# The attention products of a fused kernel: two segments a quad over two PSUM banks instead of three pairs of passes

## The chip, the cores and the metric

The kernel runs on one core of a Trainium2 chip. The metric is the device time of one execution in microseconds; lower is better.

## The reference

Attention over 8 batches, 8 heads, 576 queries and 16 + 576 keys (16 "beacon" keys in front, always visible; the rest causal), then a feed-forward network (FFN) whose hidden layer is the maximum of three products:

```python
k_all = concatenate([beacon_k, k], axis=2); v_all = concatenate([beacon_v, v], axis=2)
scores = q @ k_all.T / sqrt(64)                 # B=8, H=8, S=576, D=64
a = softmax(where(causal, -1e9, scores))        # key n of k is seen by queries >= n
attn_out = a @ v_all
x = attn_out.transpose(0, 2, 1, 3).reshape(4608, 512)
h = maximum(maximum(x @ w1, x @ w2), x @ w3)    # 512 -> 768
return h @ w_out                                # 768 -> 512, float32
```

## The kernel before, in words

**Quads.** Four heads of one batch are a quad; there are 16 quads (`Q`), two a batch. Scores are computed transposed, keys on the partitions: five key tiles `t` of 128, 128, 128, 128 and 80 keys, of which tile `t` is seen by the queries from `q_min[t]` = 0, 112, 240, 368, 496 up to 576. One quad has 1664 visible columns a head (576 + 464 + 336 + 208 + 80).

**Steps.** The visible columns are packed into bursts of at most 512 columns. The main loop in `emit_all` has one step a burst, 55 in all, numbered `k`. Quads 0 to 3 have four bursts each, packed one by one. From quad 4 on (`N_APART`) bursts run on across quads; quad 4 begins at step 16 (`late`). A step issues, in this order:

- a part of the products of an earlier quad (`emit_pv`), if one is due;
- the score products of its burst (`emit_scores`, L272; four heads side by side on four row strips of TensorE, two halves of the head dimension), into two PSUM tiles `sc` of two banks, one for two heads;
- on ScalarE the exponential of the first two heads (`emit_exp(0)`, L287), one FFN unit, the exponential of the other two, and the causal masks on GpSimd (L303);
- the planned work of that step: transposes of later q and k on VectorE (`turn`, L199), loads, casts of v on GpSimd (L225), each followed by an FFN unit if one is allowed; then the remaining allowed FFN units.

**FFN units.** `mm1_unit` multiplies a block of 512 tokens by 128 columns of one of the three weights: four products of 512 columns (eight of 256 for block 4) into an `ffn_psum` tile. Weight 0 is copied into `hT` by ScalarE (L382, a "copy" unit), weights 1 and 2 are folded in by VectorE (L387, a "maximum" unit). `mm2_unit` is an "output" unit: six products (L394) and a copy `y` on VectorE (L402). `ffn_psum` has two buffers, so the third unit of a run waits until the first is emptied. How many units a step gets follows from rates in `emit_all` (2.6 units a step at first, 3.4 later) and from `ready`, the last batch whose attention is complete.

**Attention products (PV).** A pass (`pv_pass`) covers one half of the queries (288) and one part: part 0 multiplies by ones and gives the softmax's denominators, parts 1 and 2 multiply by the even and odd columns of v. Four heads go side by side on four column strips of TensorE (L333), summed over key tiles into a PSUM tile `pv` of one bank; the pool has two. After part 0, ScalarE makes the reciprocal as the exponential of minus the logarithm (L343, L345). After parts 1 and 2, VectorE multiplies the tile by the reciprocal into `xT` (L349), the FFN's input. The passes of a quad go in three pairs, one pair a step:

```python
            [(Q, 0, 0), (Q, 1, 0)],
            [(Q, 0, 1), (Q, 0, 2)],
            [(Q, 1, 1), (Q, 1, 2)],
```

So the first pair (32 products) is followed by two logarithms and two reciprocals; the second (24) and third (40) by two multiplies each, with reciprocals that are one or two steps old. On TensorE such a step reads: PV run, score run, FFN run.

**Queues.** Every engine works its queue in the order of issue. TensorE's first score product of a step waits for the exponentials of the step before, which empty `sc`. When the loop ends, the tail issues the pairs that are left (quad 14's third and quad 15's three, each with an FFN unit before and behind) and then all units that are left, over `ffn_psum` and `sc_psum` in turn.

Of the kernel before, what the change touches and what calls it, by code (L numbers as in the profile page):

```python
# [7 lines left out]
FP32 = mybir.dt.float32  # L8
BF16 = mybir.dt.bfloat16
U32 = mybir.dt.uint32  # L10
AF = mybir.ActivationFunctionType
ALU = mybir.AluOpType
PSUM = bass.MemoryType.PSUM
# [3 lines left out]
def kernel(  # L17
# [13 lines left out]
    nc = tc.nc  # L31

    B, H, S, D = q.shape
    Nb = beacon_k.shape[2]
    NK = S + Nb
    scale = 1.0 / float(D) ** 0.5
# [8 lines left out]
    HG = 4  # L45
    n_quad = H // HG
# [5 lines left out]
    HALF = S // 2  # L52

    n_kt = (NK + 127) // 128
    k_rows = [min(128, NK - 128 * t) for t in range(n_kt)]
    q_min = [max(0, 128 * t - Nb) for t in range(n_kt)]
# [5 lines left out]
    BANK = 512  # L62
    N_APART = 2 * n_quad
    by_burst = [
        [[(0, 0, HALF), (3, q_min[3], S)], [(1, q_min[1], S)], [(2, q_min[2], S)]]
        + [[(0, HALF, S), (4, q_min[4], S)]],
        [[(0, 0, HALF), (1, q_min[1], S), (2, q_min[2], S), (0, HALF, S)]]
        + [[(3, q_min[3], S), (4, q_min[4], S)]],
    ]
    bursts = []  # L70
    at_piece = {}
    for Q in range(NQ):
# [4 lines left out]
        for group in by_burst[0 if apart else 1]:  # L77
            if apart:
                room = 0
            for t, q0, q1 in group:  # L80
                at_piece.setdefault((Q, t), []).append((q0, q1, pos))
                while q0 < q1:
# [3 lines left out]
                    w = min(room, q1 - q0)  # L86
                    bursts[-1].append((Q, t, q0, q0 + w, pos))
                    pos, q0, room = pos + w, q0 + w, room - w
# [5 lines left out]
    RING = 4  # L94
# [6 lines left out]
    xT = xt_pool.tile([128, n_ct, RING * S], BF16)  # L101
# [6 lines left out]
    nrm_pool = ctx.enter_context(tc.tile_pool(name="nrm", bufs=2))  # L108
    ffn_h = ctx.enter_context(tc.tile_pool(name="ffn_h", bufs=2))
    ffn_y = ctx.enter_context(tc.tile_pool(name="ffn_y", bufs=3))  # L110
    sc_psum = ctx.enter_context(tc.tile_pool(name="sc_psum", bufs=2, space=PSUM))
    pv_psum = ctx.enter_context(tc.tile_pool(name="pv_psum", bufs=2, space=PSUM))
    ffn_psum = ctx.enter_context(tc.tile_pool(name="ffn_psum", bufs=2, space=PSUM))

    ones = const.tile([128, 32], BF16, name="ones")
    nc.vector.memset(ones, 1.0)
# [89 lines left out]
    v_tiles = {}  # L206
# [48 lines left out]
    at = {}  # L255
# [41 lines left out]
    def emit_masks(k):  # L297
        for Q, t, q0, q1, a in bursts[k]:
            edge = min(q1, 128 * t - Nb + k_rows[t])
            if edge > q0:  # L300
                n = k_rows[t]
                view = at[Q][0:n, :, a : a + edge - q0]
                nc.gpsimd.affine_select(  # L303
                    out=view,
                    in_=view,
                    compare_op=ALU.is_ge,
                    fill=0.0,
                    base=q0 - (128 * t - Nb),
                    pattern=[[0, HG], [1, edge - q0]],
                    channel_multiplier=-1,  # L310
                )
# [3 lines left out]
    def pv_pass(Q, hf, part):  # L315
        b, g = divmod(Q, n_quad)
        at_sb, v_sb = at[Q], v_tiles[b]
        h0, h1 = hf * HALF, (hf + 1) * HALF
        runs = []
        for t in range(n_kt):  # L320
            for q0, q1, a in at_piece[Q, t]:
                lo, hi = max(q0, h0), min(q1, h1)
                if lo < hi:
                    runs.append((t, lo, hi, a + lo - q0))
        ps = pv_psum.tile([128, HALF], FP32, name="pv")
        for i, (t, lo, hi, a) in enumerate(runs):
            n = k_rows[t]
            for j in range(HG):
                if part == 0:
                    lhsT = ones[0:n, :]  # L330
                else:
                    lhsT = v_sb[0:n, t, HG * g + j, part - 1 : D : 2]
                nc.tensor.matmul(  # L333
                    ps[32 * j : 32 * j + 32, lo - h0 : hi - h0],
                    lhsT,
                    at_sb[0:n, j, a : a + hi - lo],
                    start=(i == 0),
                    stop=(i == len(runs) - 1),
                    tile_position=(0, 32 * j),
                )  # L340
        if part == 0:
            lnd = nrm_pool.tile([128, HALF], FP32, name="lnd")
            nc.scalar.activation(out=lnd, in_=ps, func=AF.Ln)  # L343
            recip = nrm_pool.tile([128, HALF], FP32, name="recip")
            nc.scalar.activation(out=recip, in_=lnd, func=AF.Exp, scale=-1.0)  # L345
            recips[Q, hf] = recip
        else:
            c0 = b % RING * S + h0
            nc.vector.tensor_mul(xT[:, 2 * g + part - 1, c0 : c0 + HALF], ps, recips[Q, hf])  # L349


    def pv_pairs(Q):
        return [
            [(Q, 0, 0), (Q, 1, 0)],
            [(Q, 0, 1), (Q, 0, 2)],
            [(Q, 1, 1), (Q, 1, 2)],
        ]

    def emit_pv(passes):
        for one in passes:  # L360
            pv_pass(*one)

# [75 lines left out]
    def emit_ffn(limit, ready, pool=None, name="fps"):  # L438
        if done[0] + 1 <= limit and done[0] < len(units) and units[done[0]][0] <= ready:
            _, fn, args = units[done[0]]  # L440
            fn(*args, pool or ffn_psum, name)
            done[0] += 1
            return True
        return False
# [15 lines left out]
    def begin():  # L460
        load_first_beacon_k(0, nc.scalar)
        load_qk(0, 1, (0, SH, QS))
        load_qk(0, 0, (0, SH, QS))
        load_qk(1, 1, (0, QS))
        load_qk(1, 0, (0, QS))
        load_first_beacon_k(1, nc.sync)
        load_v(0)
        load_beacon_k(1, 2, nc.sync)
        for which, s0, s1 in ((1, 0, SH), (1, SH, QS), (0, 0, SH), (0, SH, QS)):
            cast_qk(0, which, by_act, s0, s1)  # L470
            if (which, s0) == (0, SH):
                turn_first_beacon_k(0)
            turn(0, which, s0, s1)
        cast_qk(1, 1, by_dve)
        turn(1, 1, 0, SH)
        turn(1, 1, SH, QS)
        turn_first_beacon_k(1)
        cast_qk(1, 0, by_pool)
# [16 lines left out]
    for Q in range(2, NQ):  # L495
        b, g = divmod(Q, n_quad)
# [16 lines left out]
    def emit_all():  # L513
        begin()
        ready = -1
        allowed = 0.0


        late = first_step[2 * n_quad]
        early_rate = 2  # L520
        first_rate, rate = 2.6, 3.4
        pairs = []
        for k in range(N_STEP):
            Q = bursts[k][0][0]
            if k == late:

                while pairs:
                    emit_pv(pairs.pop(0))
                    emit_ffn(n_ft * 3, ready)
                ready = 1  # L530
                allowed += 2
            pair = ()
            if k == n_quad * 4:
                pair = pairs.pop(0)
            elif pairs and k < late and k % 4 > 0:
                pair = pairs.pop(0)
            elif pairs and k > max(late, last_step[pairs[0][0][0]] + 1):

                pair = pairs.pop(0)

            if Q >= n_quad:
                emit_pv(pair)
            emit_exp = emit_scores(k)
            if k > late and pair and pair[-1][0] % n_quad == n_quad - 1 and pair[-1][1:] == (1, 2):
                ready = pair[-1][0] // n_quad
            if k >= late:
                allowed += rate if ready > 1 else first_rate
            elif k >= n_quad * 4:
                allowed += early_rate

            emit_exp(0)
            emit_ffn(allowed, ready)
            emit_exp(1)
            emit_masks(k)
            if Q < n_quad:
                emit_pv(pair)
            if k == n_quad * 4:
                while pairs:
                    emit_pv(pairs.pop(0))
                ready = 0  # L560
            for fn in plan.pop(k, ()):
                fn()
                emit_ffn(allowed, ready)
            while emit_ffn(allowed, ready):
                pass
            if k == last_step[Q]:
                pairs += pv_pairs(Q)
        assert not plan, list(plan)
        for pair in pairs:
            emit_ffn(len(units), B - 2)  # L570
            emit_pv(pair)
            emit_ffn(len(units), B - 2)
        i = 0
        tail = [(ffn_psum, "fps"), (sc_psum, "sc")]
        while emit_ffn(len(units) - 1, B - 1, *tail[i % 2]):
            i += 1
        last_unit(*units[-1][2], (tail[i % 2], tail[(i + 1) % 2]))

    with tc.manual_schedule():
        emit_all()  # L580
# [30 lines left out]
```

## Time and profile before

| | us |
|---|---|
| median of 3 runs | 294.62 |
| lowest and highest | 294.28, 294.78 |
| profiled execution, whole | 294.3 |
| its span in the profile | 292.6 |

Of the span TensorE is busy 94%, VectorE 58%, ScalarE 54%, GpSimd 30%, at full granted clock. In the profile PE is TensorE, DVE VectorE, ACT ScalarE and POOL GpSimd. A row of a timeline has the start in the span, the length, the engine, the line of the kernel, the operation, output and input, the count, and in brackets the idle time before it and what ended that. A row of a group has busy time and mean length in ns after the first bar. A row of the waits has, after who waited for whom, the total, the number of times and the longest. A row of a window table has, for each engine, busy time and number of instructions, then the granted clock.

### The profile page before, as it was taken

How to read it: one execution, taken by the hardware profiler on the slowest of the kernel's cores; microseconds unless marked ns; L12 is line 12 of the kernel's file. 1: busy time of each engine (PE TensorE's matmuls, PEld its weight loads, DVE VectorE, ACT ScalarE, POOL GpSimd, SP SyncE). 2: the span in 40 equal slices, each digit the busy share in tenths (PEclk: the TensorE clock that was granted, in tenths of full speed). 3: DMA queues.
4: the chain of work that ended last, by engine and by line, in shares of the span. 5: the costliest groups of instructions: out<-in, count | busy, mean ns of one | idle time of the engine just before them, and what ended most of it. 6: DMA issues, size and time to landing. Idle time of an engine off the chain costs nothing.

```text
span 292.6 us, 8225 instructions
## 1 busy us (share of the span) xinstructions
PE 275.1 (94%) x3534; PEld 141.6 (48%) x3534; DVE 169.8 (58%) x297; ACT 157.2 (54%) x246; POOL 88.5 (30%) x165
## 2 busy tenths in 40 slices
PE   0697999999999999999999999999999999999995
PEld 0245445544455454545546777445454554444442
DVE  2717769756656565756646566657552545555553
ACT  5698575467872848368563756384828430220210
POOL 0474862235624423153323441332132200000000
PEclk9999999999999999999999999999999999999999
DMA  7899999589935944259057905390031002103003
GB/s 246 223 176 208 131 182 199 90 181 228 210 59 157 211 76 81 75 142 182 2 83 216 176 3 83 121 193 4 0 110 38 2 0 107 39 0 138 7 1 143
DMA packets 51924, 33.08 MB, mean 113 GB/s; under 512 B 41264, under 2 KB 42288, under 8 KB 51888
## 3 DMA queue, kind: packets, MB, share of 16 engines
q1 hardware_dynamic: 41152, 20.40, 26.5%
q0 software_dynamic: 10464, 12.01, 25.8%
q8 instruction: 27, 0.44, 0.6%
q10 hardware_dynamic: 272, 0.15, 0.2%
q14 instruction: 9, 0.07, 0.1%
HBM read 35.13 MB, written 9.44 MB: 152 GB/s over the span
## 4 chain that ended last, share of the span: by engine, by line
PE 84%; ACT 10%; DVE 2%; DMA 2%; issue 1%; SPq 0%; DVEq 0%
PE fps L374 40%; PE fps L394 14%; PE pv L333 12%; PE sc L272 10%; PE sc L374 5%; ACT at_sb L287 5%; PE sc L394 2%; ACT lnd L343 2%; DMA st<-in_q_dram 2%; ACT recip L345 1%; ACT hT L382 1%; DVE qT L199 1%; DVE hT L387 0%; DVE xT L349 0%; SPq L182 0%
## 5 line engine op out<-in xcount | busy, mean ns | idle before, releaser
L374 PE MATMUL fps<-xT,w_sb 128*128 128x512 bf16 (+1 forms) x648 | 138.6, 356 | 1.5 <-ACT hT L382 1.3
L287 ACT ACTIVATE at_sb<-sc 128x1024 bf16<-128x1024 f32 (+7 forms) x128 | 104.3, 863 | 60.6 <-PE sc L272 60.4
L387 DVE TENSOR_TENSOR hT<-hT,fps 128x512 bf16<-128x512 bf16 x96 | 65.8, 686 | 70.5 <-PE fps L374 50.4
L374 PEld LDWEIGHTS <-w_sb 128*128 128x128 bf16 x720 | 66.5, 98 | 71.1 <-issue 10.5
L303 POOL TENSOR_SCALAR_AFFINE_SELECT at_sb<-at_sb 128x512 bf16<-128x512 bf16 (+5 forms) x89 | 47.6, 551 | 132.8 <-ACT at_sb L287 124.4
L272 PE MATMUL sc<-qT,kT 32*128 32x288 bf16 (+16 forms) x1056 | 41.6, 260 | 11.7 <-DVE qT L199 9.3
L382 ACT CAST hT<-fps 128x512 bf16<-128x512 f32 x42 | 24.7, 587 | 41.8 <-PE fps L374 41.8
L394 PE MATMUL fps<-w_out_sb,hT 128*128 128x512 bf16 x180 | 41.8, 379 | 0.0
L272 PEld LDWEIGHTS <-kT 32*128 32x128 bf16 x1056 | 21.7, 94 | 28.6 <-issue 13.3
L402 DVE COPY y<-fps 128x512 f32<-128x512 f32 x30 | 20.8, 692 | 19.9 <-PE fps L394 19.8
L349 DVE TENSOR_TENSOR xT<-pv,recip 128x288 bf16<-128x288 f32 x64 | 27.0, 450 | 9.1 <-PE pv L333 8.8
L394 PEld LDWEIGHTS <-hT 128*128 128x128 bf16 x210 | 19.9, 98 | 24.4 <-DVE hT L387 1.6
L333 PE MATMUL pv<-at_sb,v_sb 128*32 128x288 bf16 (+4 forms) x1024 | 29.3, 256 | 0.4 <-DVE xT L349 0.4
L333 PEld LDWEIGHTS <-v_sb 128*32 128x32 bf16 (+1 forms) x1024 | 21.6, 97 | 14.3 <-issue 11.1
L199 DVE STREAM_TRANSPOSE kT<-c 128x256 uint32<-128x256 uint32 (+1 forms) x32 | 22.0, 706 | 3.5 <-ACT c L192 3.4
L199 DVE STREAM_TRANSPOSE qT<-c 128x256 uint32<-128x256 uint32 (+1 forms) x32 | 21.8, 706 | 0.8 <-ACT c L192 0.8
L374 PE MATMUL sc<-xT,w_sb 128*128 128x512 bf16 x72 | 18.5, 379 | 0.0
L343 ACT ACTIVATE lnd<-pv 128x288 f32<-128x288 f32 x32 | 12.9, 403 | 7.1 <-PE pv L333 7.1
L333 PE MATMUL pv<-at_sb,ones 128*32 128x288 bf16 (+4 forms) x512 | 15.2, 261 | 0.6 <-DVE xT L349 0.6
L225 POOL CAST v_sb<-vst 128x1024 bf16<-128x1024 f32 (+1 forms) x18 | 15.7, 894 | 0.1
L345 ACT ACTIVATE recip<-lnd 128x288 f32<-128x288 f32 x32 | 14.2, 444 | 1.0
L333 PEld LDWEIGHTS <-ones 128*32 128x32 bf16 (+1 forms) x512 | 10.6, 98 | 8.5 <-issue 5.2
(35 smaller groups left out, 67.9 us busy)
## 6 DMA issues: line engine op xcount, KB each, us to landing
out_dram<-y SPq DMA_DIRECT2D x35, 256.0 KB, 2.0
vst<-in_v_dram SPq DMA_DIRECT2D x21, 256.0 KB, 4.9
c<-in_k_dram POOLq DMA_DIRECT2D x14, 288.0 KB, 5.3
c<-in_q_dram POOLq DMA_DIRECT2D x14, 288.0 KB, 6.2
w_sb<-in_moe_w_dram POOLq DMA_DIRECT2D x3, 768.0 KB, 9.0
vst<-in_v_dram SPq DMA_DIRECT2D x7, 224.0 KB, 3.7
vst<-in_v_dram SPq DMA_DIRECT2D x7, 160.0 KB, 5.9
w_out_sb<-in_moe_w_out_dram POOLq DMA_DIRECT2D x1, 768.0 KB, 10.8
```

The source lines that it names most:

```text
L199: nc.vector.transpose(dst.rearrange("p (t s) -> p s t", s=RUN)[:, s0:s1], src.rearrange("p (s d) -> p s d", d=DP),)
L272: nc.tensor.matmul(sc[h // 2][:, h % 2, off : off + w], kT[hs, 128 * t : 128 * (t + 1), j], qT[hs, q0:q1, j], start=(j == 0), stop=(j == 1 ...
L287: nc.scalar.activation(out=at[Q][:, 2 * i : 2 * i + 2, a0 : a0 + w], in_=sc[i][:, :, off : off + w], func=AF.Exp, scale=scale,)
L303: nc.gpsimd.affine_select(out=view, in_=view, compare_op=ALU.is_ge, fill=0.0, base=q0 - (128 * t - Nb), pattern=[[0, HG], [1, edge - q0]], ...
L333: nc.tensor.matmul(ps[32 * j : 32 * j + 32, lo - h0 : hi - h0], lhsT, at_sb[0:n, j, a : a + hi - lo], start=(i == 0), stop=(i == len(runs) ...
L343: nc.scalar.activation(out=lnd, in_=ps, func=AF.Ln)
L349: nc.vector.tensor_mul(xT[:, 2 * g + part - 1, c0 : c0 + HALF], ps, recips[Q, hf])
L374: nc.tensor.matmul(ps[:, o0 : o0 + n], w_in[i][:, ct, 128 * ft : 128 * (ft + 1)], xT[:, ct, x0 : x0 + n], start=(ct == 0), stop=(ct == n_c ...
L382: nc.scalar.copy(hT[:, ft, :], ps)
L387: nc.vector.tensor_max(hT[:, ft, :], hT[:, ft, :], ps)
L394: nc.tensor.matmul(ps, hT[:, ft, 128 * tt : 128 * (tt + 1)], w_out_sb[:, ft, :], start=(ft == 0), stop=(ft == n_ft - 1),)
L402: nc.vector.tensor_copy(y, ps)
```

## The change

For quads 4 to 15 the three pairs become two segments, one a step: queries 0 to 240 and queries 240 to 576 (`SPLIT = q_min[2]`). A segment holds all three parts, side by side in one PSUM tile of two banks (`pv2`, one buffer in place of the two of `pv`, whose pool is closed ahead of it). In segment 0 part 0 lies at columns 0 to 240, part 1 at 240 to 480 and part 2 in the second bank; in segment 1 they lie at 0, 336 and 672, and part 1 is cut where it crosses into the second bank. Segment 0 has 24 products (key tiles 0 and 1), segment 1 has 76. TensorE posts one semaphore a segment, at its last product; the logarithm waits for that. The two multiplies (`finish`) are issued after the step's first exponential, and `ready` rises after them. The scores of these quads are packed tile by tile, so that key tile 0 is one piece and not two halves; there are 960 score products instead of 1056. Quads 0 to 3 keep their passes. The steps keep their FFN units; the steps that held a third pair have no PV run now. On TensorE's queue there are 135 unbroken runs of one kind (PV, scores, FFN), against 149.

```diff
-        [[(0, 0, HALF), (1, q_min[1], S), (2, q_min[2], S), (0, HALF, S)]]
-        + [[(3, q_min[3], S), (4, q_min[4], S)]],
+        [[(t, q_min[t], S) for t in range(n_kt)]],
...
+    def pv_segment(Q, seg):
+        b, g = divmod(Q, n_quad)
+        at_sb, v_sb = at[Q], v_tiles[b]
+        h0, h1 = ((0, SPLIT), (SPLIT, S))[seg]
+        n = h1 - h0
+        offs = (0, n, BANK) if seg == 0 else (0, n, 2 * n)
+        if len(pv_pool) == 1:
+            pv_stack.close()
+            pv_pool.append(ctx.enter_context(tc.tile_pool(name="pv2_psum", bufs=1, space=PSUM)))
+        pv_banks = pv_pool[1].tile([128, 2 * BANK], FP32, name="pv2")
+        for part in range(3):
+            runs = []
+            for t in range(n_kt):
+                ((q0, q1, a),) = at_piece[Q, t]
+                lo = max(q0, h0)
+                c = offs[part] + lo - h0
+                c1 = offs[part] + n
+                while lo < h1 and c < c1:
+                    w = min(c1, (c // BANK + 1) * BANK) - c
+                    runs.append((t, c, w, a + lo - q0))
+                    lo, c = lo + w, c + w
+            for i, (t, c, w, a) in enumerate(runs):
+                r = k_rows[t]
+                for j in range(HG):
...
+                    nc.tensor.matmul(
+                        pv_banks[32 * j : 32 * j + 32, c : c + w],
+                        lhsT,
+                        at_sb[0:r, j, a : a + w],
+                        start=(t == 0),
+                        stop=all(x[1] // BANK != c // BANK for x in runs[i + 1 :]),
+                        tile_position=(0, 32 * j),
+                    )
+        lnd = nrm_pool.tile([128, S - SPLIT], FP32, name="lnd")[:, 0:n]
+        nc.scalar.activation(out=lnd, in_=pv_banks[:, 0:n], func=AF.Ln)
+        recip = nrm_pool.tile([128, S - SPLIT], FP32, name="recip")[:, 0:n]
+        nc.scalar.activation(out=recip, in_=lnd, func=AF.Exp, scale=-1.0)
+        c0 = b % RING * S + h0
+
+        def finish():
+            for part in (1, 2):
+                nc.vector.tensor_mul(
+                    xT[:, 2 * g + part - 1, c0 : c0 + n],
+                    pv_banks[:, offs[part] : offs[part] + n],
+                    recip,
+                )
+
+        return finish
...
     def pv_pairs(Q):
+        if Q >= N_APART:
+            return [[(Q, 0)], [(Q, 1)]]
...
+            finish = None
             if Q >= n_quad:
-                emit_pv(pair)
+                finish = emit_pv(pair)
             emit_exp = emit_scores(k)
-            if k > late and pair and pair[-1][0] % n_quad == n_quad - 1 and pair[-1][1:] == (1, 2):
-                ready = pair[-1][0] // n_quad
...
             emit_exp(0)
+            if finish:
+                finish()
+                if pair[-1][0] % n_quad == n_quad - 1 and pair[-1][1] == 1:
+                    ready = pair[-1][0] // n_quad
             emit_ffn(allowed, ready)
             emit_exp(1)
...
         for pair in pairs:
             emit_ffn(len(units), B - 2)
-            emit_pv(pair)
+            emit_pv(pair)()
             emit_ffn(len(units), B - 2)
```

More of the change, by code (lines that the diff above doesn't have):

```diff
@@ L111 @@
     sc_psum = ctx.enter_context(tc.tile_pool(name="sc_psum", bufs=2, space=PSUM))
-    pv_psum = ctx.enter_context(tc.tile_pool(name="pv_psum", bufs=2, space=PSUM))
     ffn_psum = ctx.enter_context(tc.tile_pool(name="ffn_psum", bufs=2, space=PSUM))
+    pv_stack = ExitStack()
+    pv_pool = [pv_stack.enter_context(tc.tile_pool(name="pv_psum", bufs=2, space=PSUM))]
     ones = const.tile([128, 32], BF16, name="ones")
@@ L324, in pv_pass @@
                     runs.append((t, lo, hi, a + lo - q0))
-        ps = pv_psum.tile([128, HALF], FP32, name="pv")
+        ps = pv_pool[0].tile([128, HALF], FP32, name="pv")
         for i, (t, lo, hi, a) in enumerate(runs):
@@ L341, in pv_pass @@
         if part == 0:
-            lnd = nrm_pool.tile([128, HALF], FP32, name="lnd")
+            lnd = nrm_pool.tile([128, S - SPLIT], FP32, name="lnd")[:, 0:HALF]
             nc.scalar.activation(out=lnd, in_=ps, func=AF.Ln)
-            recip = nrm_pool.tile([128, HALF], FP32, name="recip")
+            recip = nrm_pool.tile([128, S - SPLIT], FP32, name="recip")[:, 0:HALF]
             nc.scalar.activation(out=recip, in_=lnd, func=AF.Exp, scale=-1.0)
@@ L349, in pv_pass @@
             nc.vector.tensor_mul(xT[:, 2 * g + part - 1, c0 : c0 + HALF], ps, recips[Q, hf])
+    SPLIT = q_min[2]
+    def pv_segment(Q, seg):
[22 more added lines that the diff above has]
+                for j in range(HG):
+                    if part == 0:
+                        lhsT = ones[0:r, :]
+                    else:
+                        lhsT = v_sb[0:r, t, HG * g + j, part - 1 : D : 2]
+                    nc.tensor.matmul(
[19 more added lines that the diff above has]
+        return finish
@@ L359, in emit_pv @@
     def emit_pv(passes):
+        if len(passes) == 1:
+            return pv_segment(*passes[0])
         for one in passes:
```

## The prediction

> **What bounds the kernel now.** First the page's busy times, then a window table over the stretch in which the changed products run, then the waits of that stretch.
>
> ```profile
> PE 275.1 (94%) x3534; PEld 141.6 (48%) x3534; DVE 169.8 (58%) x297; ACT 157.2 (54%) x246; POOL 88.5 (30%) x165
> ```
>
> ```profile
> 66.00:241.00 175.00, 173.07 (x2536) 93.26 (x2532) 102.14 (x176) 107.20 (x173) 58.34 (x110) 1.00 0.47 102
> ```
>
> ```profile
> PE fps L374 <- ACT hT L382: 1.3, 5, 0.3
> PE sc L272 <- ACT at_sb L287: 0.4, 1, 0.4
> ```
>
> From 66 to 241 us, where nearly all products of quads 4 to 15 lie, TensorE is busy 173.07 of 175 us at a granted clock of 1.00; VectorE (102.14) and ScalarE (107.20) have room. The waits that end on TensorE in this stretch are few: five for ScalarE's copies into `hT`, one for the exponentials. So what TensorE saves here comes off the end, and what makes it wait is added. Since a matmul's end is modelled, I use starts: the time from the start of one run of products to the start of the next.
>
> **Part 1, fewer and longer runs on TensorE.** The timeline of TensorE shows runs of PV (L333), score (L272) and FFN products (L374, L394):
>
> ```profile
> 83.63 0.90 PE L333 MATMUL pv<-at_sb,ones 128*32 128x288 bf16 x32
> 84.46 0.64 PE L272 MATMUL sc<-qT,kT 32*128 32x320 bf16 x16
> 85.03 1.90 PE L374 MATMUL fps<-xT,w_sb 128*128 128x512 bf16 x8
> ...
> 88.45 0.63 PE L333 MATMUL pv<-at_sb,v_sb 128*32 128x288 bf16 x24
> 89.01 0.64 PE L272 MATMUL sc<-qT,kT 32*128 32x96 bf16 x32
> 89.58 4.06 PE L394 MATMUL fps<-w_out_sb,hT 128*128 128x512 bf16 x18
> 93.57 1.18 PE L333 MATMUL pv<-at_sb,v_sb 128*32 128x288 bf16 x40
> 94.68 0.63 PE L272 MATMUL sc<-qT,kT 32*128 32x160 bf16 x16
> 95.25 2.76 PE L374 MATMUL fps<-xT,w_sb 128*128 128x512 bf16 x12
> 97.94 0.90 PE L333 MATMUL pv<-at_sb,ones 128*32 128x288 bf16 x32
> 98.78 0.64 PE L272 MATMUL sc<-qT,kT 32*128 32x112 bf16 x24
> 99.35 0.39 PE L374 MATMUL fps<-xT,w_sb 128*128 128x512 bf16 x1
> ```
>
> 18 FFN products take 89.58 to 93.57 (3.99), 12 take 95.25 to 97.94 (2.69): 1.30/6 = 0.217 us a product of 512 columns, 0.423 ns a column, and 0.09 left for the change from FFN to PV. The three PV runs of a quad take 0.83 (32 products, 8 sets of four heads, 1664 columns a head), 0.56 (24, 1024 columns) and 1.11 (40, 2304 columns). Less 0.423 ns a column that leaves 0.126, 0.127 and 0.135: about 0.113 a run and 0.002 a set. So a quad costs 2.50 now; after, with segments of 24 products (1104 columns) and 76 (3888), 4992 columns make 2.11, two runs 0.23 and 25 sets 0.05: 2.39. Twelve quads save 12 x 0.11 = 1.3. The step that lost its PV run goes from FFN straight to scores; I take that change as dear as FFN to PV. In the tail no scores follow, and two FFN-to-PV changes go as well: 0.2. Together **-1.5**.
>
> The score products are 96 fewer (24 sets), since key tile 0 is one piece. The runs of 16, 24 and 32 above take 0.57 each: **0**. The Trainium skill speaks differently (TensorEngine Tiling (Array Packing), Instruction Overhead): each matmul has about 60 cycles of overhead. At 0.423 ns a column that would be an estimated 25 ns, for 48 products fewer in all (96 gone, 48 more in PV) -1.2 us, and the sum below would be -3.1. The trace disagrees: 32 score products would need 0.8 us at that price and take 0.57.
>
> **Part 2, ScalarE's work is spread over two steps.** Steps are numbered as the loop index `k`; unit order follows from the rates and is the same in both kernels. Now a step with the first pair does two logarithms and two reciprocals ahead of its exponentials. Step 27:
>
> ```profile
> 98.41 0.41 ACT L343 ACTIVATE lnd<-pv 128x288 f32<-128x288 f32 x1 [0.57 <-PE pv L333]
> 98.49 1.59 POOL L225 CAST v_sb<-vst 128x1024 bf16<-128x1024 f32 x2
> ...
> 98.85 0.45 ACT L345 ACTIVATE recip<-lnd 128x288 f32<-128x288 f32 x1
> 99.20 0.39 ACT L343 ACTIVATE lnd<-pv 128x288 f32<-128x288 f32 x1
> ...
> 99.63 0.44 ACT L345 ACTIVATE recip<-lnd 128x288 f32<-128x288 f32 x1
> 99.98 1.01 ACT L287 ACTIVATE at_sb<-sc 128x1024 bf16<-128x1024 f32 x1
> ...
> 100.88 0.58 ACT L382 CAST hT<-fps 128x512 bf16<-128x512 f32 x1
> ...
> 101.51 1.02 PE L374 MATMUL fps<-xT,w_sb 128*128 128x512 bf16 x4 [0.26 <-ACT hT L382]
> ...
> 102.46 0.37 PE L333 MATMUL pv<-at_sb,v_sb 128*32 128x288 bf16 x5
> ```
>
> The exponential starts 1.20 after the score run (98.78), the copy of the first FFN unit follows, and the third unit, which needs that buffer, starts 1.53 after the exponential. The FFN run takes 99.35 to 102.46, 3.11 against 2.69 for twelve unhindered products: 0.42 lost. That is one of the five waits above; they are the first-pair steps whose first unit is a copy and which have three or more units (27, 37, 40, 50, 53).
>
> After, one logarithm and one reciprocal of 240 columns stand there. Call T the start of the score run behind a segment. The logarithm started 0.27 after the start of its pass's last set (97.94 + 464 columns = 98.14); with the wider last set of a segment that is T + 0.14, for either segment. Widths are scaled by the exponential's two sizes:
>
> ```profile
> L287 ACT ACTIVATE at_sb<-sc 128x1024 bf16<-128x1024 f32 x60 | 59.5, 1021 | 33.7 <-PE sc L272 33.7
> ...
> L345 ACT ACTIVATE recip<-lnd 128x288 f32<-128x288 f32 x32 | 14.2, 444 | 1.0
> L343 ACT ACTIVATE lnd<-pv 128x288 f32<-128x288 f32 x32 | 12.9, 403 | 7.1 <-PE pv L333 7.1
> ...
> L287 ACT ACTIVATE at_sb<-sc 128x512 bf16<-128x512 f32 x12 | 6.2, 602 | 2.6 <-PE sc L272 2.6
> ```
>
> 419 ns for 512 columns, 0.82 ns a column: 0.04 less for 240 and 0.04 more for 336. From start to start the rows give 0.44 (logarithm to reciprocal) and 0.35 (reciprocal to what follows); for 240 columns 0.40 and 0.31. The exponential starts at T + 0.85, not T + 1.20; the third unit could start at T + 0.85 + 1.53 = T + 2.38 and TensorE gets there at T + 0.57 + 8 x 0.217 = T + 2.30. So 0.08 is lost instead of 0.42, five times: **-1.7**.
>
> One more wait goes. In step 22 the scores wait for the exponentials of step 21:
>
> ```profile
> 75.66 1.04 ACT L287 ACTIVATE at_sb<-sc 128x1024 bf16<-128x1024 f32 x1
> ```
>
> ```profile
> 76.06 0.25 PE L272 MATMUL sc<-qT,kT 32*128 32x176 bf16 x2
> 76.75 0.63 PE L272 MATMUL sc<-qT,kT 32*128 32x176 bf16 x22 [0.44 <-ACT at_sb L287]
> 77.32 0.39 PE L374 MATMUL fps<-xT,w_sb 128*128 128x512 bf16 x1
> ```
>
> The run takes 1.26 instead of 0.57. After, that exponential ends 0.35 sooner and a PV run of 1.76 stands ahead of the scores instead of 0.56: the wait is covered by 1.5 us. **-0.7**.
>
> **Part 3, the added wait.** The reciprocals are ready two steps ahead of the multiplies now. After, both multiplies of a segment wait, at the head of VectorE's queue, for a logarithm that waits for the whole segment. Queued behind them are the maxima into `hT` that empty `ffn_psum` (two buffers), and TensorE's third unit waits for the first of these.
>
> ```profile
> 78.39 0.69 DVE L387 TENSOR_TENSOR hT<-hT,fps 128x512 bf16<-128x512 bf16 x1 [0.68 <-PE fps L374]
> ```
>
> ```profile
> 89.17 0.81 DVE L349 TENSOR_TENSOR xT<-pv,recip 128x288 bf16<-128x288 f32 x2
> ```
>
> ```profile
> L349 DVE TENSOR_TENSOR xT<-pv,recip 128x288 bf16<-128x288 f32 x64 | 27.0, 450 | 9.1 <-PE pv L333 8.8
> ```
>
> Two multiplies take 0.81 and one 0.45, so 0.36 from start to start; for 336 columns 0.42. Segment 1: logarithm T + 0.14, reciprocal T + 0.62, its end T + 1.10; with 0.05 from engine to engine (copy's end 101.46, TensorE 101.51) the multiplies start at T + 1.15 and VectorE is free at T + 1.99. The first unit's maximum could start 1.07 after its unit (77.32 to 78.39), at T + 0.57 + 1.07 = T + 1.64. It is 0.35 late; its buffer is free at T + 1.99 + 0.69 + 0.05 = T + 2.73, TensorE is there at T + 2.30 and lost 0.08 already. This takes 0.35 in each step whose first unit is a maximum and whose third follows two FFN units of four products: 22, 35, 41, 48, 54, **1.75**. In step 28 the first unit is a copy: exponential at T + 1.01, third unit T + 2.54 instead of T + 2.30, **0.25**. In 25, 38 and 51 the first unit is an output unit (six products, 1.30), ready after T + 2.0; in 31 and 44 the second is, and the third begins at T + 2.74: nothing. Segment 0 (240 columns) frees VectorE at T + 1.64: nothing. Sum **+2.0**, with 0 as its lower end (the maxima were late for another reason) and no upper end in the trace but ScalarE's own queue (first rival).
>
> At nothing I cost three things. The one PSUM tile: a segment's first product waits for the second multiply before it, at about T + 1.7 behind segment 0, and TensorE comes back at T + 2.4 at the earliest in the loop; in the tail, between the segments of quad 15, eight FFN products (1.73 + 0.09) leave 0.1. The values: segment 0 reads them a step sooner, but only key tiles 0 and 1; the cast that is as late as 98.49 is that of tiles 2 to 4, used in step 28. The end: behind the last segment stand 242 FFN products, of which 198 need it; the 44 others cover 9.5 us.
>
> Sum: -1.5 - 1.7 - 0.7 + 2.0 = **-1.9**. The profiled execution took 294.3 us around its span of 292.6; 294.3 - 1.9 = 292.4. It lies 0.3 under the median of the runs, 294.62, so the forecast there is **292.7**.
>
> **Rivals.** *Drain-bound, slower.* If the logarithm has to stand behind ScalarE's own queue (an exponential of 1.02 or a copy of 0.58), everything behind it slips. Each 0.1 costs it in eleven steps (five with a maximum and step 28 at segment 1, five with a copy at segment 0), 1.1 in all; from 0.23 on the kernel is slower by over 0.2%, at 0.3 it takes 292.7 + 3.3 = 296.0. For it: Part 3 leaves no slack. Against it:
>
> ```profile
> ACT lnd L343 <- PE pv L333: 7.1, 11, 1.3
> ```
>
> 11 of 32 logarithms waited for TensorE; the second of a pair seldom can, so of the 16 first ones most found ScalarE idle. The Trainium skill has this rival as a rule (TensorEngine Tiling (Array Packing), PSUM Bottleneck): tiling quickens TensorE but not the emptying of PSUM, which may then bound. Chance 0.21.
>
> *ScalarE's gain does not come.* If the five steps of Part 2 keep their 0.42, because the first copy is held by something else, -1.7 goes: 292.7 + 1.7 = 294.4, within 0.2% (0.59 us, about what a measurement here can tell) of 294.62. Against it: the rows of step 27 follow each other without a gap. Chance 0.15.
>
> *VectorE's wait costs nothing.* 292.7 - 2.0 = 290.7. For it: VectorE idles 42% of the time. Chance 0.10. That the change does not do what it says has no chance: the changed program's order holds 24 segments.
>
> **How the numbers follow.** Forecast 0.54 and the last rival make faster 0.64; same 0.15; slower 0.21. The range reaches below to half of the cheap case (291.0) and above almost to the drain-bound case (295.8).
>
> **What would show it.** Right: PV runs of about 0.6 and 1.76; FFN waits on ScalarE's copies down from 0.42 to about 0.1; no score wait in step 22; multiplies at T + 1.15; new waits of TensorE on VectorE of about 0.35 in steps 22, 35, 41, 48, 54. Wrong: logarithms starting over 0.2 later than T + 0.14, score runs that wait for exponentials, or PV runs that begin with a wait for the multiply.

## The result, and the profile after

| | before | after |
|---|---|---|
| median, same chip, us | 294.7 | 292.25 |
| lowest and highest, us | 294.28, 294.93 | 292.14, 292.90 |
| runs | 4 | 4 |
| span of the profiled execution, us | 292.6 | 290.6 |

The ratio is 0.9923 with a 95% interval of 0.9904 to 0.9942: the changed kernel is faster by 0.8%, 2.4 us. In its source the PV products of quads 4 to 15 are at L385, FFN products at L436 and L456, the logarithm and reciprocal at L394 and L396, the multiplies at L401, copies at L444, maxima at L449.

The page's busy times, the window of 66 to 241 us, and two rows of TensorE's waits in it:

```profile
PE 272.6 (94%) x3452; PEld 139.4 (48%) x3486; DVE 170.3 (59%) x297; ACT 157.6 (54%) x246; POOL 89.0 (31%) x165
```

```profile
66.00:241.00 175.00, 172.04 (x2512) 91.80 (x2535) 104.82 (x180) 107.71 (x174) 59.73 (x111) 1.00 0.46 104
```

```profile
PE fps L436 <- DVE hT L449: 1.1, 5, 0.2
...
PE sc L273 <- DVE qT L200: 0.2, 1, 0.2
```

TensorE still sets the end. The waits on ScalarE (five on the copies, one on the exponentials) are gone from this list, and five on VectorE's maxima stand in their place. The list undercounts: a wait shorter than the modelled tail of the product before it does not show as idle. So the steps are compared by starts, with the prediction's own prices: a step's *loss* is the time from its score run to the next run that is not FFN, less 0.57 for the scores, 0.2167 (1.30/6) a product of 512 columns and 0.09. Losses are in us.

| step | before | after | what the prediction says of it |
|---|---|---|---|
| 27, 37, 40, 50, 53 (copy first) | 0.43, 0.43, 0.45, 0.42, 0.42 | 0.06, 0.06, 0.17, 0.14, 0.14 | -1.7; measured -1.6 |
| 22 | 0.76 | 0.38 | -0.7 + 0.35; measured -0.38 |
| 35, 41, 48, 54 (maximum first) | 0.09, 0.17, 0.21, 1.01 | 0.40, 0.39, 0.39, 1.25 | +1.4; measured +0.95 |
| 28 | 0.14 | 0.22 | +0.25; measured +0.07 |
| 31, 44 (maximum, then outputs) | 0.00, 0.01 | 0.18, 0.18 | 0; measured +0.35 |
| 30 | 0.44 | 0.07 | 0; measured -0.36 |
| 23, 24, 36, 43, 49 | 0.04, 0.29, 0.04, 0.17, 0.04 | 0.00, 0.22, 0.00, 0.11, 0.00 | 0; measured -0.27 |
| all steps from 16 on | 7.08 | 5.88 | -0.4; measured -1.2 |

(Step 54's figure holds 0.87 for an FFN unit of the tail that joins its run, and the sum holds 0.63 for transposes that step 19's scores wait for; both are the same in both kernels.)

The runs on TensorE, from the timeline of steps 26 and 27:

```profile
95.34 2.76 PE L436 MATMUL fps<-xT,w_sb 128*128 128x512 bf16 x12
98.03 0.34 PE L385 MATMUL pv<-at_sb,ones 128*32 128x240 bf16 x8
98.20 0.49 PE L385 MATMUL pv<-at_sb,v_sb 128*32 128x240 bf16 x16
98.62 0.63 PE L273 MATMUL sc<-qT,kT 32*128 32x400 bf16 x16
```

Segment 0 takes 98.03 to 98.62, 0.59; segment 1 takes 1.80 (76.06 to 77.86 in step 22). That is 2.39 a quad against 2.50; over all twelve quads the PV runs sum to 28.68 us against 30.04.

ScalarE in step 27, the step that the prediction showed:

```profile
98.74 0.37 ACT L394 ACTIVATE lnd<-pv 128x240 f32<-128x240 f32 x1 [0.82 <-PE pv L385]
99.14 0.40 ACT L396 ACTIVATE recip<-lnd 128x240 f32<-128x240 f32 x1
99.45 1.01 ACT L288 ACTIVATE at_sb<-sc 128x1024 bf16<-128x1024 f32 x1
100.36 0.58 ACT L444 CAST hT<-fps 128x512 bf16<-128x512 f32 x1
```

With T = 98.62 the logarithm starts at T + 0.12, the exponential at T + 0.83 and the copy at T + 1.74. Before they were at T - 0.37 (the first of two logarithms), T + 1.20 and T + 2.10.

VectorE behind segment 1, step 22, T = 77.86:

```profile
77.98 0.45 ACT L394 ACTIVATE lnd<-pv 128x336 f32<-128x336 f32 x1 [1.09 <-PE pv L385]
78.47 0.48 ACT L396 ACTIVATE recip<-lnd 128x336 f32<-128x336 f32 x1
...
78.98 0.92 DVE L401 TENSOR_TENSOR xT<-pv,recip 128x336 bf16<-128x336 f32 x2 [1.48 <-ACT recip L396]
79.82 0.68 DVE L449 TENSOR_TENSOR hT<-hT,fps 128x512 bf16<-128x512 bf16 x1
...
80.55 1.02 PE L436 MATMUL fps<-xT,w_sb 128*128 128x512 bf16 x4 [0.21 <-DVE hT L449]
```

The multiplies start at T + 1.12, the maximum at T + 1.96 with no idle time before it, and TensorE's third unit at T + 2.69, 0.05 after the maximum's end, where it could have started at T + 2.30.

### The profile page after: what moved, and what is told of

It is laid out like the page before. It is cut to its first block, busy times and chain, and to the rows that moved or that the text cites. A ratio compares the mean times of both kernels' runs of the same rounds, so it can differ in the third digit from the quotient of the medians.

```text
span 290.6 us, 8109 instructions
## 1 busy us (share of the span) xinstructions
PE 272.6 (94%) x3452; PEld 139.4 (48%) x3486; DVE 170.3 (59%) x297; ACT 157.6 (54%) x246; POOL 89.0 (31%) x165
## 4 chain that ended last, share of the span: by engine, by line
PE 86%; ACT 5%; DVE 4%; issue 2%; DMA 2%; SPq 0%; DVEq 0%
PE fps L436 40%; PE fps L456 14%; PE sc L273 11%; PE pv L385 10%; PE sc L436 6%; PE pv L334 4%; ACT at_sb L288 2%; PE sc L456 2%; DMA st<-in_q_dram 2%; DVE hT L449 1%; DVE xT L401 1%; ACT recip L396 1%; ACT lnd L394 1%; DVE qT L200 1%; DVE xT L350 0%
## 5 line engine op out<-in xcount | busy, mean ns | idle before, releaser
L436 PE MATMUL fps<-xT,w_sb 128*128 128x512 bf16 (+1 forms) x614 | 134.3, 354 | 2.8 <-DVE hT L449 1.1
L436 PEld LDWEIGHTS <-w_sb 128*128 128x128 bf16 x720 | 66.7, 98 | 72.1 <-issue 11.6
L449 DVE TENSOR_TENSOR hT<-hT,fps 128x512 bf16<-128x512 bf16 x95 | 65.0, 685 | 40.1 <-PE fps L436 34.7
L304 POOL TENSOR_SCALAR_AFFINE_SELECT at_sb<-at_sb 128x512 bf16<-128x512 bf16 (+6 forms) x89 | 48.0, 556 | 131.5 <-ACT at_sb L288 123.3
L273 PE MATMUL sc<-qT,kT 32*128 32x288 bf16 (+15 forms) x960 | 41.7, 271 | 10.8 <-DVE qT L200 9.0
L444 ACT CAST hT<-fps 128x512 bf16<-128x512 f32 x41 | 24.0, 586 | 37.2 <-PE fps L436 35.7
L456 PE MATMUL fps<-w_out_sb,hT 128*128 128x512 bf16 x174 | 41.3, 379 | 0.5 <-issue 0.3
L401 DVE TENSOR_TENSOR xT<-pv,recip 128x240 bf16<-128x240 f32 (+1 forms) x48 | 19.7, 453 | 32.9 <-ACT recip L396 32.6
L456 PEld LDWEIGHTS <-hT 128*128 128x128 bf16 x210 | 19.8, 98 | 25.7 <-DVE hT L449 2.0
L394 ACT ACTIVATE lnd<-pv 128x240 f32<-128x240 f32 (+1 forms) x24 | 9.9, 411 | 31.2 <-PE pv L385 31.1
L385 PE MATMUL pv<-at_sb,v_sb 128*32 128x160 bf16 (+7 forms) x864 | 21.5, 243 | 0.0
L436 PE MATMUL sc<-xT,w_sb 128*128 128x512 bf16 x78 | 20.3, 379 | 0.1
L385 PEld LDWEIGHTS <-v_sb 128*32 128x32 bf16 (+1 forms) x864 | 16.3, 96 | 1.3
L449 DVE TENSOR_TENSOR hT<-hT,sc 128x512 bf16<-128x512 bf16 x13 | 8.9, 688 | 7.0 <-PE sc L436 5.2
L385 PE MATMUL pv<-at_sb,ones 128*32 128x336 bf16 (+4 forms) x336 | 13.0, 268 | 0.0
L385 PEld LDWEIGHTS <-ones 128*32 128x32 bf16 (+1 forms) x336 | 6.7, 95 | 10.4 <-issue 7.4
```

Source lines behind the costliest of these rows:

```text
L273: nc.tensor.matmul(sc[h // 2][:, h % 2, off : off + w], kT[hs, 128 * t : 128 * (t + 1), j], qT[hs, q0:q1, j], start=(j == 0), stop=(j == 1 ...
L304: nc.gpsimd.affine_select(out=view, in_=view, compare_op=ALU.is_ge, fill=0.0, base=q0 - (128 * t - Nb), pattern=[[0, HG], [1, edge - q0]], ...
L385: nc.tensor.matmul(pv_banks[32 * j : 32 * j + 32, c : c + w], lhsT, at_sb[0:r, j, a : a + w], start=(t == 0), stop=all(x[1] // BANK != c / ...
L401: nc.vector.tensor_mul(xT[:, 2 * g + part - 1, c0 : c0 + n], pv_banks[:, offs[part] : offs[part] + n], recip,)
L436: nc.tensor.matmul(ps[:, o0 : o0 + n], w_in[i][:, ct, 128 * ft : 128 * (ft + 1)], xT[:, ct, x0 : x0 + n], start=(ct == 0), stop=(ct == n_c ...
L444: nc.scalar.copy(hT[:, ft, :], ps)
```

## The experiments

Each kernel was run in five rounds beside the kernel before, which took 294.7, 294.4 and 294.8 us in the three groups (scores, spread, later and four multiplies; two tiles, deferred and extra run; output buffers and 288).

**The scores' order alone** (the kernel before with the new packing of the bursts):

```diff
-        [[(0, 0, HALF), (1, q_min[1], S), (2, q_min[2], S), (0, HALF, S)]]
-        + [[(3, q_min[3], S), (4, q_min[4], S)]],
+        [[(t, q_min[t], S) for t in range(n_kt)]],
```

> The kernel before with one edit of the change alone: key tile 0 of quads 4 to 15 is one piece, so 960 score products (240 sets of four) instead of 1056; three pairs and all else as before. Theory A (products cost by columns and by runs, not by their number): no difference, 294.6 within 0.3 us, score runs still 0.57 us. Theory B (each product has a price of its own, 25 ns): 96 products fewer, up to 2.4 us faster, about 292.2, which would be the whole gain of the change.

Measured 294.7, ratio 1.001 (0.9992 to 1.0028). 96 products fewer are worth nothing that can be measured; a price of 25 ns a product is refuted here.

**The passes spread over the three pairs** (the kernel before, its PSUM tiles and halves kept):

```diff
-            [(Q, 0, 0), (Q, 1, 0)],
-            [(Q, 0, 1), (Q, 0, 2)],
+            [(Q, 0, 0), (Q, 0, 1)],
+            [(Q, 0, 2), (Q, 1, 0)],
             [(Q, 1, 1), (Q, 1, 2)],
```

> The kernel before with only ScalarE's logarithms and reciprocals of quads 4 to 15 spread over two steps: pairs (half 0 part 0, half 0 part 1), (half 0 part 2, half 1 part 0), (half 1 parts 1 and 2); three PV runs a quad as before, two one-bank tiles. Theory A (the waits on ScalarE's copies and the score wait of step 22 are a term by themselves): five FFN runs lose no 0.42 us, step 22 no 0.69: 2.0 + 0.7 gained, up to 0.2 lost in step 28, about 292.1. Theory B (the gain of the change comes from fewer runs and score products alone): no difference, 294.6.

Measured 298.48, ratio 1.012 (1.009 to 1.0149): slower than either theory. The waits of TensorE name a cost that neither had:

```profile
PE pv L333 <- POOL v_sb L225: 5.0, 5, 1.3
```

Part 1 of half 0 needs the values of key tile 2 a step sooner than in the kernel before, and in the first quad of five of the six batches (steps 21, 27, 40, 47 and 53) GpSimd has not cast them yet. ScalarE's term did come: the five copy-first steps lost 0.27 to 0.43 less each, step 22 lost 0.69 less, and all losses fell from 7.08 to 4.52. Since two things moved at once, the term had to be tried again without the casts.

**ScalarE's steps moved, and nothing else** (the kernel before; the second half's logarithm and reciprocal go behind the step's second exponential):

```diff
+            def divide():
...
+            if hf == 1 and Q >= n_quad:
+                held.append(divide)
+            else:
+                divide()
...
             emit_exp(1)
+            while held:
+                held.pop()()
```

> The kernel before with one thing moved: in a quad's first pair, the logarithm and reciprocal of the second half go on ScalarE behind the second exponential of the step instead of ahead of the first. No product moves, nor does any VectorE multiply. Theory A (the copies of FFN's units and the next scores waited for these two ScalarE steps): the losses of steps 27, 37, 40, 50 and 53 fall by 0.3 to 0.4 each and that of step 22 by 0.69, in sum 2.4: 294.6 - 2.4 = 292.2; if step 30's loss, too, hangs on ScalarE, another 0.36 less, 291.9. Rival B (the changed kernel's gain lies in its fewer TensorE runs alone): no difference, 294.6.

Measured 293.16, ratio 0.9943 (0.9924 to 0.9963). The five copy-first steps lose 0.42, 0.43, 0.27, 0.28 and 0.28 less, 1.68 in all, and step 22's score wait (0.68) is gone. The kernel stays 1.0 above the expectation because a wait takes the place of the score wait, in step 22's PV run:

```profile
PE pv L334 <- ACT lnd L346: 0.7, 1, 0.7
```

```profile
75.98 0.42 ACT L346 ACTIVATE lnd<-pv 128x288 f32<-128x288 f32 x1
...
76.44 0.41 PE L334 MATMUL pv<-at_sb,v_sb 128*32 128x288 bf16 x12 [0.70 <-ACT lnd L346]
```

The held logarithm still reads one of the two `pv` tiles when the next pass wants it. That run takes 1.45 instead of 0.56; -1.68 - 0.68 + 0.89 and +0.22 in steps 35 and 48 make -1.25, against 1.2 measured. Step 30's loss stays 0.44, so it does not hang on the two steps of ScalarE that were moved.

**Eleven more runs on TensorE** (the kernel before; the second pass of each third pair goes behind the scores, ten times from step 16 on and once in step 15, for quad 2, which the expectation does not count):

```diff
+            split = Q >= n_quad and pair and pair[0][1:] == (1, 1)
             if Q >= n_quad:
-                emit_pv(pair)
+                emit_pv(pair[:1] if split else pair)
             emit_exp = emit_scores(k)
+            if split:
+                emit_pv(pair[1:])
```

> The kernel before with the second pass of each third pair (10 steps, 23 to 52) issued behind the step's score products instead of ahead of them: the same products, 10 more runs of TensorE between kinds of product. Theory A (a change of kind costs about 0.11 us each): 294.6 + 10 x 0.11 = 295.7. Rival B (the 0.11 us a quad came from another thing, such as the widths of the products): 294.6.

Measured 295.99, ratio 1.0044 (1.0028 to 1.006), that is +0.8 to +1.8 us. The timeline of step 23:

```profile
81.22 0.68 PE L333 MATMUL pv<-at_sb,v_sb 128*32 128x288 bf16 x20
81.83 0.67 PE L272 MATMUL sc<-qT,kT 32*128 32x32 bf16 x24
82.43 0.68 PE L333 MATMUL pv<-at_sb,v_sb 128*32 128x288 bf16 x20
83.04 1.25 PE L374 MATMUL fps<-xT,w_sb 128*128 128x512 bf16 x5
```

The two passes take 0.61 each, 1.22, where they took 1.11 in one run: 0.11 for the same products in one more run. The ten steps from 23 to 52 all show it, no other step changes, and from step 16 on the profile is 1.06 us longer than that of the kernel before.

**The multiplies a unit later** (the changed kernel; `finish` goes behind the step's first FFN unit):

```diff
-            if finish:
-                finish()
...
             emit_ffn(allowed, ready)
+            if finish:
+                finish()
...
```

> The changed kernel with the two multiplies issued behind the step's first FFN unit, so that its maximum stands ahead of them in VectorE's queue. Theory A (the multiplies that wait for the reciprocal hold up that maximum, and TensorE's third unit by 0.2 to 0.35 us, in seven steps): those waits go, 1.2 to 1.7 us faster than the changed kernel, about 290.8. Theory B (the wait costs nothing, or the maxima are late for another reason): the same as the changed kernel, 292.3.

Measured 293.96, ratio 0.9972 (0.9955 to 0.9989): slower than the changed kernel, a miss. Steps 22, 31 and 44 lost 0.29, 0.14 and 0.13 less, as expected, and steps 39, 24, 30, 43, 41 and 54 lost 0.78, 0.70, 0.43, 0.42, 0.33 and 0.32 more. The waits of TensorE:

```profile
PE fps L436 <- DVE hT L449: 0.8, 3, 0.4
PE sc L273 <- DVE qT L200: 0.7, 2, 0.5
PE fps L436 <- DVE y L464: 0.6, 1, 0.6
PE fps L456 <- DVE hT L449: 0.6, 1, 0.6
```

The multiplies now stand ahead of the next unit's maximum, an output's copy or a transpose, which were in time before. Moving VectorE's wait in its queue only hands it on.

**Each multiply done twice** (the changed kernel):

```diff
-            for part in (1, 2):
+            for part in (1, 2, 1, 2):
```

> The changed kernel with each segment's two multiplies done twice (same result): VectorE is free 0.84 us later behind a segment 1 and 0.65 later behind a segment 0. Theory A (each 0.1 us by which the multiplies end later is paid by TensorE): seven segment-1 steps whose first unit is a maximum lose 0.84 more, three whose first is an output unit about 0.35, five segment-0 steps whose first is a maximum 0.65: 5.9 + 1.0 + 3.2, about 10 us slower than the changed kernel, 302. Theory B (VectorE, idle 41% of the time, takes it up): within 1 us of the changed kernel.

Measured 304.24, ratio 1.0329 (1.03 to 1.0358), 12 us over the changed kernel. VectorE is only 59% busy in the changed kernel, but time at this place in its queue is paid by TensorE:

```profile
PE fps L436 <- DVE hT L449: 6.6, 9, 1.0
```

The steps of the expectation's three groups lose 0.82, 0.35 and 0.56 more each, 9.6 in all. The rest was not expected: steps 28, 39, 40 and 50 lose 2.3 more.

**Two PSUM tiles a segment** (the changed kernel; products by bank, part 0 and the first piece of part 1 in the first tile):

```diff
-        pv_banks = pv_pool[1].tile([128, 2 * BANK], FP32, name="pv2")
-        for part in range(3):
+        pv_banks = [pv_pool[1].tile([128, BANK], FP32, name=f"pv_{x}") for x in "ab"]
+        for bank, part in ((0, 0), (0, 1), (1, 1), (1, 2)):
...
-        nc.scalar.activation(out=lnd, in_=pv_banks[:, 0:n], func=AF.Ln)
+        nc.scalar.activation(out=lnd, in_=pv_banks[0][:, 0:n], func=AF.Ln)
```

> The changed kernel with each segment's accumulator as two PSUM tiles of one bank each, the products ordered by bank, and the multiplies cut at the bank's edge (two of 240 in segment 0 as before; 176, 160 and 336 wide in segment 1). The logarithm of segment 1 can start when 512 of its 1008 columns are done, some 0.85 us before the segment's last product, so the reciprocals stand at about T - 0.75 + 0.95 = T + 0.2 instead of T + 1.1, and the three multiplies can end at about T + 1.2 (T: start of the score run behind the segment). Theory A (the rest of the added VectorE wait hangs on logarithm, reciprocal and multiplies in a row behind the segment's last product): the waits of steps 22, 31, 35, 41, 44, 48 and 54, +1.6 in sum against the kernel before, go, and the time is 292.25 - 1.6 = 290.6. Rival B (VectorE is late for another reason, the number of its multiplies or the drain of its own reads): the waits stay and 12 more multiplies add up to 12 x 0.1: 292.3 to 293.5.

Measured 290.18, ratio 0.9848 (0.9823 to 0.9873), below the changed kernel's interval. Step 22, T = 76.96:

```profile
76.21 0.45 ACT L392 ACTIVATE lnd<-pv_a 128x336 f32<-128x336 f32 x1 [0.30 <-PE pv_a L383]
76.70 0.48 ACT L394 ACTIVATE recip<-lnd 128x336 f32<-128x336 f32 x1
...
77.22 0.34 DVE L403 TENSOR_TENSOR xT<-pv_a,recip 128x176 bf16<-128x176 f32 x1 [0.62 <-ACT recip L394]
77.47 0.73 DVE L403 TENSOR_TENSOR xT<-pv_b,recip 128x160 bf16<-128x160 f32 x2
...
78.61 0.69 DVE L451 TENSOR_TENSOR hT<-hT,fps 128x512 bf16<-128x512 bf16 x1 [0.41 <-PE fps L438]
```

The logarithm starts at T - 0.75, VectorE is free at T + 1.24, and the maximum waits for its unit, as it should, at T + 1.65. In 66 to 239 us the only wait of TensorE left is 0.2 us for a transpose. Steps 22, 35, 41, 48 and 54 lose 0.29 to 0.31 less than in the changed kernel, 31 and 44 0.14 less, 27, 28 and 37 0.06 less; step 39 loses 0.31 more. All losses fall from 5.88 to 4.25.

**A fourth output buffer** (the two-tile version, `ffn_y` with `bufs=4`):

> The two-tile version (290.2) with four buffers instead of three for the tiles in which the output leaves. In the two-tile version a copy of an output unit in step 38/39 waited for an earlier output's transfer, and step 39 lost 0.31 us that the changed kernel does not lose. Theory A (the faster loop has run into the output buffers there): step 39's loss falls from 0.34 to 0.03, and the time by 0.3, to 289.9. Rival B (the late copy has another cause): step 39 as before, 290.2.

Measured 290.02, ratio 0.9831 (0.9807 to 0.9855), which the runs do not tell from the two-tile version. The trace does: step 39's loss is 0.03 instead of 0.34, every other step is unchanged, and VectorE's wait for an output's transfer at that place is shorter. The two-tile version's row, then this one's:

```profile
DVE y L466 <- DMA out_dram<-y: 0.9, 1, 0.9
```

```profile
DVE y L466 <- DMA out_dram<-y: 0.6, 1, 0.6
```

**The division at query 288** (the two-tile version):

```diff
-    SPLIT = q_min[2]
+    SPLIT = HALF
...
-        offs = (0, n, BANK) if seg == 0 else (0, n, 2 * n)
+        offs = (0, n, 2 * n)
```

> The two-tile version (290.2) with the quad divided at query 288 instead of 240: two segments of equal size, 2 x 3 x 288 columns, of which the first needs the values of key tile 2 as well. Theory A (the division at 240 matters because GpSimd casts key tile 2's values late): the products of the first segment wait on that cast in the first quad of each batch, steps 21, 27, 40, 47 and 53, by about 1.2 us each, as they did in the version with the passes spread over the pairs: 290.2 + 5 x 1.2 = 296. Rival B (the place of the division only balances the work of the two segments): within 0.5 of 290.2.

Measured 295.16, ratio 1.0012 (0.9995 to 1.0029): the whole gain is gone, 5.0 us. The waits, and step 21 in the timeline:

```profile
PE pv_b L383 <- POOL v_sb L226: 3.8, 5, 1.0
```

```profile
73.12 0.23 PE L383 MATMUL pv_b<-at_sb,v_sb 128*32 128x64 bf16 x8
74.38 0.43 PE L383 MATMUL pv_b<-at_sb,v_sb 128*32 128x48 bf16 x16 [1.02 <-POOL v_sb L226]
```

In five of the six batches the first segment of the first quad stops at the products of key tile 2. Elsewhere a first segment takes 0.79 (in step 34, for the first quad of the remaining batch, too); in steps 21, 27, 40, 47 and 53 it takes 2.00, 1.78, 1.76, 1.38 and 1.78, together 4.75 more.

## Why the prediction was right, point by point

Forecast 292.7, measured 292.25: a gain of 2.4 us where the sum said 1.9. That the two lie so close is in part luck: VectorE's term was 0.7 too large where the prediction put it, steps 31 and 44 cost 0.35 that it did not have, and step 30 gave 0.36 that the change was not made for.

- **Fewer and longer runs, -1.5: confirmed.** 2.39 a quad to the hundredth, and the extra-run kernel shows the same 0.11 as a cost. Of the 2.7 us that the profile gains from step 16 on (last section), the losses (1.2) and the PV runs (30.04 - 28.68) leave 0.1, too little to tell the tail's 0.2. The Trainium skill says that a change of tiling mode drains TensorE (TensorEngine Tiling (Array Packing), Key Properties) and gives no price; the runs are in keeping with that, at about 0.11 us a run, but do not show what the time goes into.
- **96 score products for nothing: confirmed** by the scores' order alone. The Trainium skill's 60 cycles a product (TensorEngine Tiling (Array Packing), Instruction Overhead) would have brought an estimated 1.2 us in the change; the trace and this run disagree, for products that run four side by side.
- **ScalarE, -1.7 and -0.7: confirmed.** -1.59 in the five steps, and the score wait of step 22 is gone. The deferred kernel shows both without any other part of the change (-1.68 and -0.68), and so rules out the rival in which the copies are held by something else. The exponential stands 0.02 earlier after T than worked out; steps 40, 50 and 53 keep 0.14 to 0.17, twice the 0.08 given, and keep as much in the deferred and the two-tile kernel.
- **VectorE, +2.0: right in mechanism, +1.32 in size where it was put.** That is 0.30 in step 22 (0.38, against 0.08 in the deferred kernel), 0.95 in steps 35, 41, 48 and 54, and 0.07 in step 28; with steps 31 and 44, below, it is +1.67. The chain (T + 0.12, 0.61, 1.12, 1.96) is within 0.03 of the one worked out, and the two-tile kernel, whose PV runs take the same 0.59 and 1.80, shortens this chain and takes 1.8 of the losses away. The step that was mis-sized is "this takes 0.35 in each": the third unit was taken to lose 0.08 in every such step before, and steps 35, 41 and 48 lost 0.09, 0.17 and 0.21; after, steps 22, 35, 41 and 48 all stand at 0.38 to 0.40. Step 28's copy cost 0.07 instead of 0.25.
- **"In 31 and 44 the second is [an output unit] ... nothing": wrong, +0.35.** The prediction looked at the buffer of the third unit. What waited is inside the second. Its sixth product reads the last column block of `hT`, which the step's first unit has just produced, so it needs the very maximum that the multiplies delay:

```profile
118.07 0.67 PE L273 MATMUL sc<-qT,kT 32*128 32x16 bf16 x24
...
120.03 0.68 DVE L449 TENSOR_TENSOR hT<-hT,fps 128x512 bf16<-128x512 bf16 x1
```

The maximum ends at 120.71; the output unit's sixth product starts at 120.77, 0.353 after the fifth instead of 0.216.

- **Step 30, -0.36: not foreseen, and luck.** In the kernel before, the step's second maximum starts 0.41 after its unit's last product ends, where others start within about 0.1; the fourth unit then waits for its buffer:

```profile
114.36 0.69 DVE L387 TENSOR_TENSOR hT<-hT,fps 128x512 bf16<-128x512 bf16 x1 [2.35 <-PE fps L374]
...
115.52 0.69 DVE L387 TENSOR_TENSOR hT<-hT,fps 128x512 bf16<-128x512 bf16 x1 [0.47 <-PE fps L374]
```

Counted in the trace with VectorE's waits for semaphores, which the timeline leaves out, this maximum is VectorE's 192nd record. In all eleven profiles together, from 40 us on, nine instructions of VectorE start more than 0.12 after all that they wait for, as far as the posts of the semaphores tell; each is a maximum, 0.37 to 0.41 late, and each is the 192nd, 320th or 448th record, places that lie 128 apart. The new score packing, the deferred logarithms and the extra run leave VectorE's order up to here, and keep the delay at the 192nd. In the changed kernel the 192nd is a wait and shows none, while the maxima at 189.46 and 271.34, its 320th and 448th, are 0.40 late; the first of them costs TensorE nothing. So the gain hangs on where an instruction falls in VectorE's program, not on fewer runs or on ScalarE. What VectorE does at these places, and why other records there are in time, no run shows.

- **The rivals.** Drain-bound did not come: in all 24 segments the logarithm starts at T + 0.12 or 0.13, not behind ScalarE's queue. That VectorE's wait costs nothing is refuted by +1.67, and by 12 us when the multiplies are doubled.
- **The one PSUM tile, at nothing: confirmed.** In the changed kernel no wait of a segment's products for the multiplies stands among TensorE's waits.
- **"Segment 0 reads them a step sooner, but only key tiles 0 and 1": this zero carried the result.** The division at 288 shows what stands behind it: 5.0 us.

The two-tile version with three or four output buffers, 290.2 and 290.0 us, beats both kernels.

## What to carry to other kernels

On an engine that is nearly always busy, count the runs between kinds of product as well as the products: here a run cost about 0.11 us, and 96 products fewer gave nothing. Before cutting work into other pieces, look up for each piece when the last of its inputs is made: here one key tile more was worth twice the gain. And a chain that starts at the end of an accumulation can start earlier if what it reads has a PSUM tile of its own; that removed a wait which reordering the queue only passed on.

## What the runs showed of the hardware

The same PV products can run at half their pace early in the execution, and in some executions longer than in others. Rows of the changed kernel, then of the kernel before, for the same work of quads 0 and 1, ahead of anything that the change touches:

```profile
24.43 2.11 PE L334 MATMUL pv<-at_sb,v_sb 128*32 128x288 bf16 x40
26.33 1.72 PE L334 MATMUL pv<-at_sb,ones 128*32 128x288 bf16 x32
```

```profile
24.20 1.18 PE L333 MATMUL pv<-at_sb,v_sb 128*32 128x288 bf16 x40
25.94 1.04 PE L333 MATMUL pv<-at_sb,ones 128*32 128x288 bf16 x32 [0.57 <-DVE xT L349]
```

In both profiles a set of four heads starts every 0.83 ns a column up to some moment and every 0.43 ns a column from then on. In the profile of the kernel before, that moment lies ahead of the first of its rows; in that of the changed kernel it lies within the second. It is the moment at which the trace's record of the granted clock begins: 22.92 us in the kernel before, 27.70 in the changed kernel, 22.7 to 28.6 in the eleven profiles. From there the record says 1.00; ahead of it there is no record, and a 1.00 that a view gives for that stretch is no measurement. The Trainium skill tells of a half-rate clock whose end varies from run to run (TensorE: Matmul & The Clock Gate, Part 1: The HAM clock gate); the traces agree in the pace, 0.83 against 0.43 ns a column, and in that the end varies, but it varies by 5.9 us here, where that section has half a microsecond either way. What ends it here, no run shows.

This is noise for the comparison, since it lies ahead of the change. Step 16's scores start at 56.09 in the profile of the changed kernel against 55.30 before, so the spans understate the gain by 0.8; from step 16 on it is 237.25 against 234.56, -2.7. In the other profiles the start lay between 54.7 and 56.4, and from step 16 on they differ from the kernel before by -0.1 (scores), +3.4 (spread), -1.2 (deferred), +1.1 (extra run), -0.3 (later multiplies), +10.6 (four multiplies), -4.4 (two tiles), -4.7 (fourth buffer) and +0.4 (288): the same order as the medians give.
